# Cluster-routed attention with a SoLU feed-forward block: the same 1,568 operations recorded in another order

## The chip, the cores and the metric

The kernel runs on one core of a Trainium2 chip. The metric is the device time of one execution in microseconds, given as the median of three runs. Beside these runs stands one profiled execution, from which all durations, waits and starts below are read.

## The reference

Two stages follow each other. With B = 4 batches, H = 8 heads, S = 768 tokens and D = 64 the first is

```python
q_assign = argmax(normalised q . normalised centroids)      # 16 clusters a head
k_assign = argmax(normalised k . normalised centroids)
mask = q_assign[:, :, :, None] == k_assign[:, :, None, :]
scores = where(mask, scale * q @ k^T, -1e9)
attn = softmax(scores) @ v
```

Its output, 3072 tokens of 512 numbers, goes through the second:

```python
h = x @ w_in                          # 512 -> 1024
solu = h * softmax(h)
ln = (solu - mean) / sqrt(var + 1e-6) * g_ln
out = ln @ w_out                      # 1024 -> 512
```

## The kernel before, in words

**Scores.** The mask is put into the score matmul: under the 64 rows of q and of k stand the one-hot rows of the clusters, so that a pair of tokens in one cluster gets a constant more. One operation S r.x (L641) fills one of the two 512-column banks of a score tile `sb`; E r (ACT, L651) takes the exponent of both, 128x1024 at once. There are 144 regions r. V n.j (L663) multiplies six 128x128 blocks of exponents by v and by a column of ones into `ob`; N g (DVE, a reciprocal at L675 and a product at L686) normalises a group of these sums into the rows x of the second stage.

**Preparation of a pair of heads, b.p.** Loads of q and k (`ld`, SP) and v (`lv`); the transposes: for batch 0 by PE (`tp`, L396) with copies out of the banks on ACT or DVE (`xa`, `xt`, L407 and L409), for the others on DVE (`xt`, L421, 128x768); the products with the centroids on PE (`cl`, L470), turned back on DVE (`tb`, L479), their maximum (`mx`, L489), the one-hot comparison (`oh`, L493) and its transpose (`ot`, L500 and L505); the placing of the one-hot rows under q and k (`pl`, L529 and L531), the casts of q and k into their wide tiles (`ca`, L437 to L441, on POOL or ACT), the blank of unused rows (`bl`, L543), the cast of v (`cv`, L554 and L556).

**Feed-forward, tile f of 24.** `tx` (an SP transpose by DMA; PE for the first two and the last tile, `ptx`, L747) turns 128 rows of x. `h f.f2.part` (L772) fills the two banks `hb`, two matmuls of 512 columns each; `hm` (DVE, L782) takes a bank out with its running maximum; `ex` (ACT, L798) is the exponent; `u` (POOL or DVE, L805) is the product of exponent and h; `tu` (SP, L811) turns it by DMA; `bn` (DVE, L816, two a tile), `as` (L835) and `ag` (DVE, L821 and L823) make the variance; `al` (POOL, L840) its power -1/2. `y f.part` (L844) fills the one bank `mb`, four parts of two matmuls; `sc` (ACT, L856, or DVE, L858) scales the bank into the output tile, and `ou` stores it. Since `mb` is one bank, y of the next tile waits for `sc` of this one. The weights w_in come in by `li` (SP, into three staging buffers) and are cast by `wi` (POOL, L580); `ce` centres w_out.

**What sets the order.** Each operation is recorded under a name with what it needs. Two tables at the top of the file decide the rest: `AWAY` puts some operations on another engine than the usual one, and `ORDER` lists all names in the order in which `Weave.run` emits them. Each engine runs its own instructions in that order and waits by semaphore for what they need. Nothing else reorders the work; SP's queue too, with its loads, DMA transposes and stores, is one line in which a waiting entry holds up those behind it.

Of the kernel before, what the change touches and what calls it, by code (L numbers as in the profile page):

```python
# [38 lines left out]
lc ld0.0.0.0 ld0.0.1.0 ld0.0.0 ld0.0.1 ld0.1.0 ld0.1.1 lv0.0 ld0.2.0 ld0.2.1 ld0.3.0 lo3 lv0.1  # L39
ld0.3.1 lg lv0.2 lo1 lo2 lo0 cx z5 cy cz wu tp0.0.0.0 tp0.0.0.1 tp0.0.1.0 tp0.0.1.1 cp xa0.0.0  # L40
xt0.0.0 xa0.0.1 xt0.0.1 tp0.1.0.0 xa0.1.0 cb cl0.0 tb0.0 mx0.0 oh0.0 ot0.0 ca0.0.0.0.0 z3
ca0.0.1.0.0 ca0.0.0.0.1 cc ca0.0.0.1.1 ca0.0.0.1.0 pl0.0.1.1 pl0.0.0.0 ca0.0.1.0.1 ca0.0.1.1.1
ca0.0.1.1.0 tp0.1.0.1 tp0.1.1.0 xt0.1.0 xa0.1.1 cl0.0.1 tp0.1.1.1 cv0.0.1 xt0.1.1 pl0.0.0.1
tp0.2.0.0 tp0.2.0.1 tb0.0.1 mx0.0.1 oh0.0.1 ot0.0.1 pl0.0.1.0.1 pl0.0.1.0.0 pl0.0.1.1.1 cl0.1 sg
pl0.0.1.1.0 z1 ca0.1.1.0 cv0.0.0 ca0.1.0.0 xa0.2.0 pl0.0.1.0 tp0.2.1.0 xt0.2.0 xa0.2.1 S0.0 S0.1
E0 tp0.2.1.1 xt0.2.1 S1.0 tp0.3.0.0 S1.1 S2.0 S2.1 tp0.3.0.1 tb0.1 mx0.1 oh0.1 xa0.3.0 E1 E2 cl0.2
xt0.3.0 S3.0 S3.1 V0.0 V0.1 V1.0 S4.0 S4.1 V1.1 tp0.3.1.0 tb0.2 E3 S5.0 S5.1 E4 E5 ot0.1 N0 mx0.2
gt tp0.3.1.1 S6.0 S6.1 V2.0 V2.1 S7.0 S7.1 V3.0 V3.1 xa0.3.1 gk xt0.3.1 cl0.3 E6 E7 cv0.1.0
pl0.1.1.1 ca0.1.0.1 ca0.3.0.0 pl0.1.1.0 ca0.3.0.1 z2 ca0.1.1.1 oh0.2 pl0.1.0.0 pl0.1.0.1 gw S8.0
S8.1 S9.0 S9.1 me0 me1 ot0.2 tb0.3 pl0.2.1.0 N1 pl0.2.0.0 mx0.3 mk oh0.3 ca0.2.0.0 ca0.2.1.0  # L50
ca0.3.1.0 ca0.2.1.1 pl0.2.1.1 pl0.2.0.1 E8 E9 ca0.2.0.1 S10.0 S10.1 S11.0 S11.1 V4.0 V4.1 V5.0
V5.1 E10 S12.0 S12.1 cv0.2.1 E11 E12 mf N2 ot0.3 pl0.3.0.0 ld1.0.0.0 li0 ld1.0.0.1 ld1.0.0.2
ld1.0.0 ld1.0.1.0 lv0.3 ld1.0.1.1 ld1.0.1.2 ld1.0.1 cv0.1.1 ca0.3.1.1 pl0.3.1.0 pl0.3.0.1 cv0.2.0
cv0.3.0 cv0.3.1 wi0 S13.0 S13.1 V6.0 V6.1 S14.0 S14.1 V7.0 V7.1 pl0.3.1.1 N3 km ce0 E13 E14 S15.0
S15.1 S16.0 S16.1 E15 E16 V8.0 V8.1 S17.0 S17.1 E17 V9.0 V9.1 S18.0 S18.1 E18 S19.0 S19.1 N4 ce5
# [1299 lines left out]
```

## Time and profile before

| what | value |
|---|---|
| median of 3 runs | 222.03 us (221.85 to 222.12) |
| the profiled execution | 222.33 us |
| its span | 220.5 us |
| instructions | 6292 |
| HBM read and written | 23.11 MB and 6.29 MB |

The span runs from the first to the last recorded instruction; 1.83 us of the profiled execution lie around it. A start such as 42.81 is counted from the start of the span. In rows of a timeline stand the start, the length, the engine, the line, the operation, what it writes and reads, and in brackets the time for which the engine stood idle before it with the work that ended this. In rows of the chain of waits stand start, length and what the chain passes through. PE stands for TensorE, DVE for VectorE, ACT for ScalarE, POOL for GpSimd, SP for SyncE. The lengths of neighbours on one engine overlap a little, so a row of several operations (x2, x13) gives the pace at which they follow each other.

### The profile page before, as it was taken

How to read it: one execution, taken by the hardware profiler on the slowest of the kernel's cores; microseconds unless marked ns; L12 is line 12 of the kernel's file. 1: busy time of each engine (PE TensorE's matmuls, PEld its weight loads, DVE VectorE, ACT ScalarE, POOL GpSimd, SP SyncE). 2: the span in 40 equal slices, each digit the busy share in tenths (PEclk: the TensorE clock that was granted, in tenths of full speed). 3: DMA queues.
4: the chain of work that ended last, by engine and by line, in shares of the span. 5: the costliest groups of instructions: out<-in, count | busy, mean ns of one | idle time of the engine just before them, and what ended most of it. 6: DMA issues, size and time to landing. Idle time of an engine off the chain costs nothing.

```text
span 220.5 us, 6292 instructions
## 1 busy us (share of the span) xinstructions
PE 211.4 (96%) x2401; PEld 148.9 (68%) x2431; DVE 185.7 (84%) x430; ACT 192.8 (87%) x245; POOL 158.8 (72%) x198
## 2 busy tenths in 40 slices
PE   7899999999999999999999999999999999999984
PEld 4567577677678776777677677666777767655442
DVE  3699979968999999896799999994888856989982
ACT  3799999999999998999999989999999888685362
POOL 3686969897898999549939997879889054456610
PEclk9999999999999999999999999999999999999999
DMA  5998999999999993999999981939584229777522
GB/s 199 394 402 259 189 175 300 126 154 259 164 154 169 190 188 62 174 248 210 153 225 162 180 184 38 171 92 209 151 173 90 72 64 168 154 120 170 163 94 100
DMA packets 120911, 38.33 MB, mean 174 GB/s; under 512 B 109993, under 2 KB 116401, under 8 KB 120881
## 3 DMA queue, kind: packets, MB, share of 16 engines
q1 hardware_dynamic: 120448, 37.40, 81.7%
q10 hardware_dynamic: 432, 0.52, 0.7%
q8 instruction: 19, 0.31, 0.6%
q14 instruction: 12, 0.09, 0.2%
HBM read 23.11 MB, written 6.29 MB: 133 GB/s over the span
## 4 chain that ended last, share of the span: by engine, by line
PE 72%; DVE 10%; DMA 6%; POOL 5%; issue 3%; ACT 2%; SPq 1%; DVEq 0%; ACTq 0%; POOLq 0%
PE sb L641 22%; PE hb L772 16%; PE mb L844 15%; PE ob L663 12%; DMA w_st<-in_moe_w_in_dram 4%; PE hb L470 3%; DMA raw<-in_q_dram 2%; DVE w_st L782 2%; PE hb L396 2%; DVE xt L421 2%; DVE bs L816 2%; POOL kbig L441 1%; PE mb L470 1%; POOL w_in_sb L580 1%; POOL v L556 1%
## 5 line engine op out<-in xcount | busy, mean ns | idle before, releaser
L651 ACT ACTIVATE e<-sb 128x1024 bf16<-128x1024 f32 x144 | 139.9, 1024 | 8.9 <-PE sb L641 8.1
L641 PE MATMUL sb<-qbig,kbig 80*128 80x256 bf16 (+3 forms) x648 | 83.8, 261 | 1.3 <-ACT e L651 1.0
L641 PEld LDWEIGHTS <-kbig 80*128 80x128 bf16 (+1 forms) x648 | 62.9, 119 | 25.4 <-issue 8.6
L805 POOL TENSOR_TENSOR u<-e_sb,w_st 128x1024 bf16<-128x1024 bf16 x21 | 45.1, 2145 | 20.0 <-ACT e_sb L798 13.3
L663 PEld LDWEIGHTS <-e 128*128 128x128 bf16 x1152 | 48.6, 97 | 10.4 <-DVE x L686 0.6
L663 PE MATMUL ob<-v,e 128*128 128x65 bf16 x1140 | 51.4, 193 | 0.2
L772 PE MATMUL hb<-w_in_sb,xT 128*128 128x512 bf16 x173 | 50.6, 379 | 0.9 <-POOL v L1323 0.3
L844 PE MATMUL mb<-w_out_c,uT 128*128 128x512 bf16 x165 | 45.5, 379 | 1.2 <-DVE y L858 0.4
L816 DVE BATCH_NORM_STATS2 bs<-u 128x6 f32<-128x512 bf16 x48 | 31.6, 680 | 1.1 <-POOL u L805 1.1
L798 ACT ACTIVATE e_sb<-w_st,nmax 128x1024 bf16<-128x1024 f32 (+1 forms) x25 | 27.8, 1113 | 3.2 <-DVE w_st L782 1.8
L439 POOL CAST qbig<-xt 64x768 bf16<-64x768 f32 (+1 forms) x31 | 25.7, 830 | 6.5 <-PE ob L663 2.7
L441 POOL TENSOR_SCALAR kbig<-xt 64x768 bf16<-64x768 f32 (+1 forms) x32 | 27.6, 865 | 2.4 <-DVE xt L409 0.8
L840 POOL TENSOR_TENSOR alpha<-var,halves 128x1 f32<-128x1 f32 x24 | 15.3, 638 | 12.6 <-DVE var L823 8.0
L421 DVE STREAM_TRANSPOSE xt<-raw 128x768 f32<-128x768 f32 x24 | 22.5, 959 | 0.1
L844 PEld LDWEIGHTS <-uT 128*128 128x128 bf16 x176 | 15.2, 97 | 10.2 <-issue 0.8
L772 PEld LDWEIGHTS <-xT 128*128 128x128 bf16 x192 | 15.8, 98 | 8.8 <-issue 0.6
L686 DVE TENSOR_TENSOR x<-ob,den 128x256 bf16<-128x256 f32 (+2 forms) x40 | 19.0, 474 | 1.4
L782 DVE TENSOR_SCALAR_CACHE_REDUCE w_st<-hb 128x512 f32<-128x512 f32 x24 | 16.3, 680 | 3.8 <-PE hb L772 3.7
L782 DVE TENSOR_SCALAR_CACHE_REDUCE w_st<-hb,nmax 128x512 f32<-128x512 f32 x24 | 17.8, 740 | 1.9 <-PE hb L772 1.5
L856 ACT ACTIVATE y<-mb,alpha 128x512 f32<-128x512 f32 x15 | 10.3, 685 | 6.5 <-POOL alpha L840 3.6
L675 DVE RECIPROCAL den<-ob 128x4 f32<-128x4 f32 (+2 forms) x40 | 7.1, 178 | 10.4 <-PE ob L663 10.1
L556 POOL CAST v<-vf 128x384 bf16<-128x384 f32 x22 | 10.9, 504 | 3.3 <-DMA vf<-in_v_dram 2.6
(109 smaller groups left out, 202.6 us busy)
## 6 DMA issues: line engine op xcount, KB each, us to landing
vf<-in_v_dram SPq DMA_DIRECT2D x16, 384.0 KB, 5.3
out_dram<-y SPq DMA_DIRECT2D x23, 256.0 KB, 2.5
raw<-in_k_dram SPq DMA_DIRECT2D x26, 192.0 KB, 4.6
raw<-in_q_dram SPq DMA_DIRECT2D x24, 192.0 KB, 5.1
w_g<-in_moe_w_out_dram SPq DMA_DIRECT2D x4, 512.0 KB, 8.7
w_st<-in_moe_w_in_dram SPq DMA_DIRECT2D x4, 512.0 KB, 8.0
raw<-in_q_dram SPq DMA_DIRECT2D x3, 384.0 KB, 6.6
...
```

The costliest lines, as they stand in the source:

```text
L421: nc.vector.transpose(xts[b, p, i][:], raw_of(b, p, i))
L439: (nc.vector if e == "DVE" else nc.gpsimd).tensor_copy(dst, src)
L441: (nc.vector if e == "DVE" else nc.gpsimd).tensor_scalar(dst, src, scalar1=inv_C, scalar2=1.0, op0=Alu.mult, op1=Alu.mult)
L641: nc.tensor.matmul(reg[:, c:c + wd], kb[u, pp, side_of(h), keys], qb[u, pp, side_of(h), su * P:su * P + wd])
L651: nc.scalar.activation(es[r][:, :w], src, Act.Exp, scale=exp_scale, bias=-exp_scale)
L663: nc.tensor.matmul(ops_of(group_of[n])[:, s, :VW], es[r][:, c0:c0 + P], v1[index[b, pair_of(h)] % R][:, side_of(h), kt, :VW], start=(kt == ...
L772: nc.tensor.matmul(hb[f2][:], xTs[f][:, dc, :], w_in_sb[:, dc, f2 * BANK:(f2 + 1) * BANK], start=(dc == 0), stop=(dc == n_dc - 1))
L782: nc.vector.tensor_scalar(ff[f, "h"][:, f2 * BANK:(f2 + 1) * BANK], hb[f2][:], scalar1=-1.0, scalar2=nmax[:, f2 - 1:f2] if f2 else 3.0e38, ...
L798: nc.scalar.activation(ff[f, "e"][:, cols(f, f2)], ff[f, "h"][:, cols(f, f2)], Act.Exp, bias=ff[f, "nmax"][:, n_ff2 - 1:], scale=-1.0, acc ...
L805: (nc.vector if e == "DVE" else nc.gpsimd).tensor_tensor(ff[f, "u"][:, cols(f, f2)], ff[f, "e"][:, cols(f, f2)], ff[f, "h"][:, cols(f, f2) ...
L816: nc.vector.bn_stats(ff[f, "bs"][:, f2, :], ff[f, "u"][:, f2 * BANK:(f2 + 1) * BANK])
L844: nc.tensor.matmul(y_of(f, x), ff[f, "uT"][:, fc, :], w_out_c[:, fc, parts_of(f, x)], start=(fc == 0), stop=(fc == n_fc - 1))
```

## The change

The two tables are replaced; all 1,568 operations, their buffers and their instructions stay. By `AWAY`, DVE has 296 operations instead of 301, ACT 216 instead of 219, POOL 191 instead of 183; PE (722) and SP (143) are as they were. In detail: of `pl`, 12 go from DVE to POOL and 5 back, 2 from ACT to POOL and 2 back, and one each way between ACT and DVE; of `cv`, 6 go from ACT to POOL and 4 back; of `ca`, 3 from ACT to POOL and one back; of `as`, 9 from DVE to POOL and 10 back; of `sc`, 3 from ACT to DVE and 4 back; of `u`, u14 and u20 go from DVE to POOL, u10, u13 and u16 back; of `bl`, one goes to POOL and two to DVE. The `ORDER` table is new throughout. A line of it before, and two of now (the scalings of tile 9 and what stands around them):

```diff
-S117.0 E116 S117.1 E117 V76.0 h15.0.0 h15.0.1 S118.0 S118.1 V76.1 ot3.2 sc9 u13.0 pl3.2.1.1
+ca3.2.0.1 pl3.2.0.1 cv3.2.0 S115.0 S115.1 S116.0 S116.1 h14.1.0 h14.1.1 V75.0 y9.1 E115 ex13.0
+E116 V75.1 V76.0 V76.1 y9.2 y9.3 S117.0 S117.1 S118.0 S118.1 V77.0 h15.0.0 E117 E118 sc9 y10.0
```

The tables of the changed kernel have one line less, so that its lines read one lower than before (L641 is L640). Three places follow, as they stand on the engine.

**ACT ahead of the first exponent.** Before, from the copy xa0.1.0 (the first transpose of pair 0.1) to E0. The cast to `kbig` is ca0.0.1.1.0, the cast to `v_0` is cv0.0.1; L529 are placings.

```order
L407 COPY xt<-hb_92 128x384
L437 ACTIVATE kbig_99<-xt 64x2x3x64
L407 COPY xt<-hb_93 128x384
L407 COPY xt<-hb_92 128x384
L554 CAST v_0_102<-vf 128x6x64
L407 COPY xt<-hb_93 128x384
L529 COPY qbig_96<-oht 32x6x32
L407 COPY xt<-hb_92 128x384
L529 COPY kbig_99<-oht 32x6x32
```

Now, from the same copy:

```order
L406 COPY xt<-hb_92 128x384
L406 COPY xt<-hb_93 128x384
L406 COPY xt<-hb_92 128x384
L406 COPY xt<-hb_93 128x384
L528 COPY qbig_96<-oht 32x6x32
L406 COPY xt<-hb_92 128x384
L528 COPY qbig_96<-oht 32x6x32
```

The two casts have left this stretch for POOL, and ca0.0.1.0.0, which POOL did, now stands on ACT three rows earlier. On SP, the loads of q and k of pair 0.2 now stand ahead of the first load of v, the last load of v ahead of the first of w_in, and li2, which stood behind li1 and li3, ahead of both; the one that takes the buffer freed by the cast wi0 is then li3.

**DVE around the scaling of tile 9.** Before, from N30 (the reciprocal and the product, 6x64) to `sc9` (L858) and three rows on:

```order
L675 RECIPROCAL den<-ob 128x6
L686 TENSOR_TENSOR x<-ob,den 128x6x64
L816 BN_STATS bs<-u 128x6
L500 STREAM_TRANSPOSE oht<-oh 128x768
L858 TENSOR_SCALAR y<-mb,alpha 128x512
L821 BN_AGGR mv<-bs 128x2
L823 TENSOR_SCALAR var<-es_2777,esum,mv 128x1
L816 BN_STATS bs<-u 128x6
```

Now, from hm14.0, two rows behind N30 (between them stands hm13.1), to `sc9` (L857):

```order
L781 TENSOR_SCALAR w_st,nmax<-hb_92 128x512
L834 TENSOR_SCALAR es_2911<-esum 128x1
L542 MEMSET kbig_100 16x2x384
L815 BN_STATS bs<-u 128x6 x2
L820 BN_AGGR mv<-bs 128x2
L822 TENSOR_SCALAR var<-es_2630,esum,mv 128x1
L820 BN_AGGR mv<-bs 128x2
L822 TENSOR_SCALAR var<-es_2783,esum,mv 128x1
L820 BN_AGGR mv<-bs 128x2
L822 TENSOR_SCALAR var<-es_2900,esum,mv 128x1
L815 BN_STATS bs<-u 128x6
L857 TENSOR_SCALAR y<-mb,alpha 128x512
```

Between N30 and `sc9` stand hm13.1, hm14.0, as12, bl3.2, bn11 twice, ag9, ag10, ag11 and bn12.0, where before there were bn10.1 and ot3.2. The last of them reads u12, which POOL makes.

**DVE ahead of the products with the centroids of pairs 3.2 and 3.3.** These are sixteen matmuls on PE, of which the last (cl3.3) reads the transpose xt3.3.1. Before, from the normalising N27 (4 columns):

```order
L675 RECIPROCAL den<-ob 128x4
L686 TENSOR_TENSOR x<-ob,den 128x2x2x64
L835 TENSOR_SCALAR es_2642<-esum 128x1
L421 STREAM_TRANSPOSE xt<-raw 128x768
L531 COPY qbig_96<-oht 32x4x192
L421 STREAM_TRANSPOSE xt<-raw 128x768 x3
```

Now, from the same N27:

```order
L674 RECIPROCAL den<-ob 128x4
L685 TENSOR_TENSOR x<-ob,den 128x2x2x64
L781 TENSOR_SCALAR w_st,nmax<-hb_92 128x512
L820 BN_AGGR mv<-bs 128x2
L822 TENSOR_SCALAR var<-es_2495,esum,mv 128x1
L781 TENSOR_SCALAR w_st,nmax<-hb_93,nmax 128x512
L420 STREAM_TRANSPOSE xt<-raw 128x768 x3
```

One transpose, one small operation and one placing have left the stretch, and hm11 of both banks and ag8 have come in.

More of the change, by code (lines that the diff above doesn't have):

```diff
@@ L35 @@
+    u8.0 u9.0
 """.split(), "POOL"))
 ORDER = """
[L39 to L55, printed above, removed]
@@ new lines @@
+h21.0.1 y17.0 y17.1 y17.2 hm20.1 ex20.0 S141.0 S141.1 E141 h21.1.0 y17.3 S142.0 S142.1 h21.1.1
+S143.0 S143.1 sc17 as18 ag18 as19 al18 hm21.0 hm21.1 E142 E143 ex21.0 y18.0 V94.0 bn19.0 as20
+y18.1 V94.1 y18.2 h22.0.0 h22.0.1 y18.3 sc18 u20.0 u21.0 bn19.1 bn20.0 bn20.1 N39 ag19 ag20 hm22.0
+h22.1.0 V95.0 V95.1 h22.1.1 hm22.1 ex22.0 al19 as21 u22.0 y19.0 ptx23.0 tx23.0 N40 y19.1 y19.2
+y19.3 ptx23.1 h23.0.0 h23.1.0 ou17 tu20 ou18 tu21 bn21.0 tx23.1 bn21.1 al20 h23.0.1 sc19 y20.0
+y20.1 y20.2 y20.3 sc20 h23.1.1 ou19 hm23.0 ag21 bn22.0 hm23.1 ptu22.0 ptu22.1 tu22.1 bn22.1 ex23.0
```

198 lines of the change are left out of this document (103 added, 95 removed).

## The prediction

> **What bounds the kernel now.** First the page's busy times:
>
> ```profile
> PE 211.4 (96%) x2401; PEld 148.9 (68%) x2431; DVE 185.7 (84%) x430; ACT 192.8 (87%) x245; POOL 158.8 (72%) x198
> ```
>
> then the same by stretches of the span:
>
> ```profile
> 12.00:45.00 33.00, 31.57 (x416) 22.66 (x414) 28.91 (x60) 32.17 (x39) 27.06 (x39) 1.00 1.01 236
> 45.00:85.00 40.00, 39.68 (x502) 30.03 (x506) 37.42 (x81) 39.28 (x47) 35.78 (x40) 1.00 1.01 174
> 125.00:165.00 40.00, 39.58 (x430) 28.30 (x437) 35.24 (x77) 37.91 (x49) 33.91 (x38) 1.00 0.77 144
> 165.00:205.00 40.00, 39.62 (x458) 26.73 (x463) 31.64 (x88) 31.52 (x41) 21.73 (x22) 1.00 0.59 123
> ```
>
> The columns behind the window are PE, its weight loads, DVE, ACT, POOL, the granted clock (1.00 throughout), DMA. In the three rows behind 45 us PE lacks 0.3 to 0.4 us of each 40: no reordering can win much there, only a new hole can lose. The others are busy for 85 to 98% in the rows up to 165 us, so a row that is moved back on DVE or ACT has little room. From 12 to 45 us ACT is busy for 32.17 of 33 us. There ACT bounds, as its timeline shows:
>
> ```profile
> 12.99 1.02 ACT L651 ACTIVATE e<-sb 128x1024 bf16<-128x1024 f32 x1
> ...
> 26.63 12.27 ACT L651 ACTIVATE e<-sb 128x1024 bf16<-128x1024 f32 x13
> 39.10 1.94 ACT L651 ACTIVATE e<-sb 128x1024 bf16<-128x1024 f32 x2 [0.19 <-PE sb L641]
> ...
> 43.94 10.76 ACT L651 ACTIVATE e<-sb 128x1024 bf16<-128x1024 f32 x11 [0.22 <-PE sb L641]
> ```
>
> Exponents follow each other at 12.27 / 13 = 0.94 us; from E0 at 12.99 to 54.7 the timeline names two holes, 0.19 and 0.22. So the time up to there is E0's start plus ACT's work. What sets E0 is read from the chain of waits in the first microseconds, followed back from a matmul at 20 us:
>
> ```profile
> 7.94 0.48 ACT xt L407
> ...
> 8.44 0.52 ACT kbig L437
> 8.96 0.77 ACT xt L407 x2
> ...
> 9.76 0.52 ACT v L554
> ...
> 10.37 0.88 PE hb L396 x6
> ```
>
> The reader is to see the two casts (ca0.0.1.1.0, cv0.0.1) inside the chain: PE's transposes of pair 0.2 at 10.37 stand behind them.
>
> **The change part by part.** The sum is made against the profiled execution, 222.33 us; the median, 222.03, lies 0.30 lower, and the result is moved by that.
>
> *ACT ahead of E0.* Both casts leave this stretch. The 0.52 and 0.52 don't come back whole: xt0.1.0 also needs its own transpose on PE, and DVE's second round of one-hots keeps its place. Carried on: xa0.1.0 ends at 8.42, xt0.1.0 can start at some 8.65, then xa0.1.1 and xt0.1.1 at about 0.45 each (0.77 for two in the chain); the transposes of pair 0.2 start at about 10.05 for 10.37. I take **-0.35**; the ends are 0 (DVE's chain is late instead) and -1.0 (both casts). What POOL gets, it has idle time for (72% busy), and the v cast isn't needed before the first values matmul. Since ACT has no hole behind E0, the gain lasts to 54.7 us.
>
> *The hole at 43.94.* PE stood before it, and behind a weight load:
>
> ```profile
> 41.72 1.04 POOL L580 CAST w_in_sb<-w_st 128x1024 bf16<-128x1024 f32 x1 [0.80 <-DMA w_st<-in_moe_w_in_dram]
> ...
> 42.81 0.38 PE L772 MATMUL hb<-w_in_sb,xT 128*128 128x512 bf16 x1 [0.33 <-POOL v L1323]
> ```
>
> The first row is the cast wi2, released by a load; PE's second matmul of h0.0.1 begins when it is done. (The releaser named, a small fill on POOL, is the one behind the cast.) The chain of waits of the whole span passes here:
>
> ```profile
> 29.84 1.85 issue
> ...
> 33.68 7.99 DMA w_st<-in_moe_w_in_dram
> ```
>
> That load, 7.99 us from 33.68, is li2, the last of three, waiting for the buffer that wi0 frees, while wi0 stood behind a late v load (the 1.85 without work in POOL's chain). Now the v load is ahead of w_in's first, and li2 goes first of the three; li3 takes the freed buffer, with the same 7.99 us from about 31, thus at 39 us. The wait goes: **-0.2**, ACT's hole of 0.22 (ends 0 and -0.4, both holes).
>
> *y2.0.* Tile 2's first matmul waited for sc1, which stood on DVE behind two transposes:
>
> ```profile
> 85.32 0.71 DVE L858 TENSOR_SCALAR y<-mb,alpha 128x512 f32<-128x512 f32 x1
> 86.08 0.38 PE L844 MATMUL mb<-w_out_c,uT 128*128 128x512 bf16 x1 [0.36 <-DVE y L858]
> ```
>
> Now sc1 stands right behind ag2 and N16 and y2.0 later: **-0.35** (ends 0 and -0.5).
>
> *y10.0.* Here a wait comes. What ran there, from the timeline:
>
> ```profile
> 155.99 0.75 DVE L858 TENSOR_SCALAR y<-mb,alpha 128x512 f32<-128x512 f32 x1 [0.67 <-PE mb L844]
> 156.66 0.20 DVE L821 BATCH_NORM_AGGREGATE mv<-bs 128x2 f32<-128x12 f32 x1
> ...
> 157.09 0.68 DVE L816 BATCH_NORM_STATS2 bs<-u 128x6 f32<-128x512 bf16 x1
> ...
> 157.90 0.59 PE L844 MATMUL mb<-w_out_c,uT 128*128 128x512 bf16 x2
> ```
>
> and the pace of work that runs back to back, from the chain of waits:
>
> ```profile
> 64.35 0.56 PE ob L663 x18
> ...
> 69.05 0.66 DVE w_st L782 x2
> ...
> 71.81 0.70 DVE kbig L543
> ...
> 75.86 1.20 DVE bs L816 x2
> ...
> 78.27 1.83 DVE xt L421 x2
> ...
> 88.85 0.44 PE sb L641 x4
> ...
> 98.74 0.86 PE hb L772 x4
> ```
>
> Before, sc9 ran at 155.99 as soon as PE was done, over 1 us ahead of y10.0 at 157.90. Now DVE has, behind the end of h14.0.1: hm14.0 0.66, as12 0.07 (an estimate, half a row), bl3.2 0.70, bn11 1.20, three ag at 157.09 - 156.66 = 0.43, bn12.0 0.60, sc9 0.75; with 0.2 to start (an estimate) and 0.05 to release PE (sc1 ended at 86.03 above, PE began at 86.08), 5.5 us. In the new table PE has in the same time h14.1, y9.1 to y9.3 and h15.0.0 (12 matmuls at 0.215), S115 to S118 (16 at 0.11) and V75 to V77.0 (30 at 0.03): 2.58 + 1.76 + 0.9 = 5.2. Difference **+0.3**. Ends: 0, and +1.0 where u12, which bn12.0 reads, is late too.
>
> *cl3.3.* From the end of V67 DVE has N27 (0.56, rows below), hm11 of both banks (1.32), ag8 0.43, three transposes at 0.91, and 0.2 to start: 5.25 us. PE has S103 to S106 (1.76), y7 (8 at 0.215, 1.72), V68 and V69 (24, 0.72) and cl3.2 (0.78): 4.95 us.
>
> ```profile
> 139.96 0.14 DVE L675 RECIPROCAL den<-ob 128x4 f32<-128x4 f32 x1
> 140.14 0.42 DVE L686 TENSOR_TENSOR x<-ob,den 128x256 bf16<-128x256 f32 x1
> ...
> 139.25 1.68 PE L470 MATMUL hb<-xt,c_bd 128*32 128x384 f32 x16
> ```
>
> (0.78 is half of the 16 products' pace.) **+0.3** (ends 0 and +0.6).
>
> *ptx23.1.* PE's last transpose of x waits for N40. From the end of h21.1.1 DVE has hm21.1, bn19 and bn20, N39, ag19, ag20, hm22, a copy and N40: by the same paces 0.66 + 2.4 + 0.45 + 0.86 + 1.32 + 0.3 + 0.45 and 0.3 for starts, 6.75 us, for 6.55 of PE (y18, h22 and y19, 24 matmuls, 5.16; S143, V94, V95 and a transpose, 1.4). Before, N40 stood two rows behind N39, ag19, ag20 and hm22 as well, but bn19 and bn20 were done by then.
>
> **+0.2** (ends 0 and +0.6). Behind it hm23.1 now stands ahead of bn22.1 (0.6 us), but y22 waits for ACT's copy, which now stands behind the exponents of tile 23: 0.
>
> *What isn't listed.* Some fifteen other places (y4.0, y14.0, S53 to S80, V66) come out within 0.1 us of PE's work, as many did before; I take **+0.3** for them, at 0.02 each, with ends -0.3 and +1.0. For DMA transposes and stores I found none whose new place on SP uses up its lead: 0.
>
> Sum: -0.35 - 0.2 - 0.35 + 0.3 + 0.3 + 0.2 + 0.3 = **+0.2**, so 222.53 for the profiled execution and **222.3 us** as a median.
>
> **The rivals.** *No new wait bites.* The three DVE chains start earlier than I have them, or rows overlap more; then only the first three terms count: -0.9, thus 221.1. For it: all three excesses are at most 0.3 us, near what these paces can tell. Against: DVE is busy for 88 and 94% of the two rows up to 165 us, with little idle time to start early from.
>
> *ACT bounds throughout.* ACT loses two casts of q or k net, two of v, and gets one scaling more:
>
> ```profile
> 41.06 0.84 ACT L437 ACTIVATE qbig<-xt 64x768 bf16<-64x768 f32 x1
> ...
> L856 ACT ACTIVATE y<-mb,alpha 128x512 f32<-128x512 f32 x15 | 10.3, 685 | 6.5 <-POOL alpha L840 3.6
> ```
>
> With 0.51 for a cast of v (9.76 in the chain above): -1.68 - 1.02 + 0.69 = -2.0, thus 220.0. Against: from 125 to 165 us ACT is idle for 2.1 us of 40, PE for 0.4. The Trainium skill, "Perfetto Trace Analysis", section "Identifying the Most-Contended Engine", says to judge PE by its weight loads (68% here) and not by matmul time, which would make ACT (87%) the engine to relieve. The stretches speak against it: score matmuls follow at 0.11 us without a gap while the weight loads stand at 30 of 40.
>
> *POOL is late for sc9.* That is the other side: sc9 now stands behind bn12.0, which waits for u12. POOL has ahead of it two casts, u11, a placing and u12:
>
> ```profile
> 153.14 2.14 POOL L805 TENSOR_TENSOR u<-e_sb,w_st 128x1024 bf16<-128x1024 bf16 x1
> ```
>
> u12 ended at 155.28. y10.0 stands at 157.9; less sc9, its release and bn12.0 (1.4 us), u12 decides from 156.5 on. POOL has eight operations more than before, and a cast of q or k holds it for 0.8 us each, as one took on ACT (41.06 above). With 1.0 more at y10.0 the time is 223.3. That engines slow each other is seen: the comparison `oh` of one size took
>
> ```profile
> 62.58 1.55 DVE L493 TENSOR_TENSOR oh<-cst,mx 128x768 bf16<-128x768 f32 x1
> 147.39 0.95 DVE L493 TENSOR_TENSOR oh<-cst,mx 128x768 bf16<-128x768 f32 x1
> ```
>
> in two places, 0.6 us apart. The Trainium skill, "SBUF — State Buffer", section "SBUF: two separate sides", has VectorE (in operations with two SBUF inputs) and GpSimd lock one port pair for a whole instruction; by that rule work moved to POOL holds DVE up as well, and this rival would be the likelier one.
>
> *The order doesn't matter.* PE hides all of it: 222.0.
>
> **How the numbers follow.** Forecast 0.44, between 221.8 and 222.8; no new wait 0.18; ACT bound 0.04; POOL late 0.27; no matter 0.07. A measurement tells 0.2%, 0.44 us, from no change. Faster than that: 0.18 + 0.04 and 0.03 of the forecast's own = 0.25. Within it: 0.07 and 0.26 of the forecast = 0.33. Slower: 0.27 and 0.15 of the forecast (the unlisted places at their upper end) = 0.42. The range goes from the no-wait rival, 221.0, to POOL late with the upper ends of the other two DVE chains, 223.3 + 0.7 = 224.0.
>
> **What would show it.** Right: E0 starts at about 12.6; no PE wait at h0.0.1 and y2.0; new PE waits of 0.2 to 0.5 on DVE at y10.0, cl3.3 and ptx23.1. Wrong: E0 at 13.0 or later; a wait of 1 us at y10.0 with u12's end behind 156.5; PE waiting on a DMA behind 45 us.

## The result, and the profile after

| | before | after |
|---|---|---|
| median of 4 runs each, on one chip | 222.07 us (221.85 to 222.16) | 223.84 us (223.43 to 224.57) |
| ratio | | 1.0086, 95% interval 1.0066 to 1.0107 |
| profiled execution, its span | 222.33, 220.5 us | 223.43, 221.7 us |

The new order is slower by 1.8 us, and by 1.1 us between the two profiled executions. The forecast was 222.3 us within 221.0 to 224.0; the sign with the larger chance came true, the size did not.

The busy times of the page and the same four stretches as before hide this well:

```profile
PE 213.2 (96%) x2431; PEld 147.8 (67%) x2431; DVE 182.4 (82%) x425; ACT 191.0 (86%) x242; POOL 162.0 (73%) x206
```

```profile
12.00:45.00 33.00, 31.96 (x423) 22.91 (x424) 29.64 (x63) 32.00 (x39) 27.29 (x37) 1.00 1.02 247
45.00:85.00 40.00, 40.00 (x495) 29.25 (x494) 37.86 (x79) 38.95 (x46) 33.79 (x38) 1.00 0.94 172
...
125.00:165.00 40.00, 39.16 (x428) 27.43 (x424) 35.26 (x82) 36.48 (x47) 31.81 (x37) 1.00 0.74 129
165.00:205.00 40.00, 40.00 (x468) 26.56 (x466) 27.37 (x77) 32.96 (x43) 20.41 (x20) 1.00 0.61 133
```

DVE and ACT have less to do than before, PE is at 40.00 of 40 in two rows, and yet the kernel is slower. The one row that became worse is 125 to 165 us: PE 39.16 for 39.58, ACT 36.48 for 37.91. PE lost more than these two numbers say. In before the trace has 2401 of the 2431 matmuls, and the 0.42 us that PE lacks in this row are eight holes of 0.05 us where a matmul's record is missing; in after all are there, and the 0.84 us are three waits (0.32, 0.15 and 0.37, below). A matmul that waits is partly counted as busy, so even this is only a part. What shows the rest is the start of the same operation in two traces. Four marks serve all kernels below: E0, E33 and E100 (exponents on ACT, where both orders have done nearly the same work) and the second matmul of y23.1.3, directly ahead of y23.0.0, which is among the last matmuls.

| profiled execution | E0 | E0 to E33 | E33 to E100 | E100 to y23.1.3 | span |
|---|---|---|---|---|---|
| before | 12.99 | 35.91 | 82.41 | 84.84 | 220.5 |
| after | 12.90 | 35.32 | 82.50 | 86.53 | 221.7 |
| blank_pool | 13.54 | 36.03 | 82.50 | 85.58 | 222.1 |
| place_dve | 12.58 | 36.04 | 82.48 | 86.35 | 221.9 |
| u10_pool | 13.01 | 36.04 | 82.48 | 85.97 | 221.9 |
| tail_norm | 13.22 | 35.99 | 82.49 | 87.07 | 223.2 |
| ce_later | 12.62 | 35.31 | 83.07 | 86.66 | 222.0 |
| pool_quiet | 12.89 | 35.30 | 82.97 | 86.52 | 222.1 |
| before_ce2 | 12.82 | 35.75 | 82.41 | 84.84 | 220.2 |
| hybrid | 12.83 | 35.43 | 82.29 | 84.99 | 219.9 |
| front_only | 12.43 | 36.03 | 82.47 | 84.96 | 220.3 |
| y10_only | 13.09 | 35.58 | 82.42 | 86.84 | 222.3 |
| tail_only | 12.69 | 36.11 | 82.41 | 85.11 | 220.7 |
| y10_three | 13.36 | 36.02 | 82.49 | 85.69 | 222.0 |

Between before and after: -0.09, -0.59, +0.09 and +1.69, together +1.10. In these two executions the front gained what it was to gain, 0.67 us by E33; behind E100 more than twice as much was lost. In most other profiled executions of this front it gained nothing from E0 to E33, as is told below under the collision.

**The front.** ACT's timeline, after:

```profile
8.81 0.86 ACT L406 COPY xt<-hb 128x384 f32<-128x384 f32 x2 [0.46 <-PE hb L395]
...
12.90 1.02 ACT L650 ACTIVATE e<-sb 128x1024 bf16<-128x1024 f32 x1
...
34.91 3.78 ACT L650 ACTIVATE e<-sb 128x1024 bf16<-128x1024 f32 x4 [0.39 <-ACT e L650]
38.99 1.94 ACT L650 ACTIVATE e<-sb 128x1024 bf16<-128x1024 f32 x2 [0.30 <-PE sb L640]
...
41.70 12.46 ACT L650 ACTIVATE e<-sb 128x1024 bf16<-128x1024 f32 x13
```

The two casts are gone, but in their place ACT waits 0.46 us for PE's transposes, and E0 came only 0.09 earlier. The last row is 13 exponents without a hole: the wait of 0.22 at 43.94 is gone, since the load that it hung on is. POOL's timeline has the cast wi2 in a row of three that starts at 37.33, where before it waited 0.80 us for its load and ran at 41.72:

```profile
37.33 3.01 POOL L579 CAST w_in_sb<-w_st 128x1024 bf16<-128x1024 f32 x3
```

**Tile 2 and pair 3.3.** PE's timeline at y2.0 and at the products with the centroids:

```profile
84.28 0.60 PE L843 MATMUL mb<-w_out_c,uT 128*128 128x512 bf16 x2
...
138.35 1.74 PE L469 MATMUL hb<-xt,c_bd 128*32 128x384 f32 x16
```

y2.0 has no bracket behind it any more: its wait is gone. The sixteen products took 1.74 for 1.68 us; the wait for DVE's last transpose, which lies inside this row, is the same in both orders.

**Around y10.0.** First DVE's timeline, after:

```profile
146.21 1.21 DVE L804 TENSOR_TENSOR u<-e_sb,w_st 128x1024 bf16<-128x1024 bf16 x1
...
152.16 0.68 DVE L781 TENSOR_SCALAR_CACHE_REDUCE w_st<-hb 128x512 f32<-128x512 f32 x1
...
153.93 0.70 DVE L542 MEMSET kbig<- 16x768 f32 x1 [1.00 <-ACT kbig L528]
154.64 1.29 DVE L815 BATCH_NORM_STATS2 bs<-u 128x6 f32<-128x512 bf16 x2
...
157.11 0.68 DVE L815 BATCH_NORM_STATS2 bs<-u 128x6 f32<-128x512 bf16 x1
157.71 0.73 DVE L857 TENSOR_SCALAR y<-mb,alpha 128x512 f32<-128x512 f32 x1
```

and one row of the same engine before, at the same operation hm14.0 as the second row above:

```profile
152.45 0.69 DVE L782 TENSOR_SCALAR_CACHE_REDUCE w_st<-hb 128x512 f32<-128x512 f32 x1 [2.54 <-PE hb L772]
```

Before, DVE stood idle for 2.54 us here, waiting for PE's h14.0.1. After, hm14.0 comes as promptly behind it, but the idle time has been filled, with u10 (1.21, which POOL did before) among others, and the statistics that could have gone ahead now stand behind. In between bl3.2, which blanks rows behind the placings of its tile, waits 1.00 us for the placing pl3.2.1.0, which is on ACT now; sc9, the last row, ends at 158.44. ACT and PE, after:

```profile
149.72 1.15 ACT L797 ACTIVATE e_sb<-w_st,nmax 128x1024 bf16<-128x1024 f32 x1 [0.68 <-POOL u L804]
...
152.81 0.83 ACT L528 COPY kbig<-oht 32x768 f32<-32x768 f32 x1
```

```profile
151.65 0.38 PE L771 MATMUL hb<-w_in_sb,xT 128*128 128x512 bf16 x1
...
152.84 0.60 PE L640 MATMUL sb<-qbig,kbig 96*128 96x256 bf16 x4 [0.32 <-ACT e L650]
...
156.92 0.60 PE L640 MATMUL sb<-qbig,kbig 80*128 80x256 bf16 x4 [0.15 <-ACT e L650]
...
158.50 0.59 PE L843 MATMUL mb<-w_out_c,uT 128*128 128x512 bf16 x2 [0.37 <-DVE y L857]
```

The first row is the end of h14.0.1, 152.03. From there to y10.0 PE waits three times, at S116.1, S118.1 and y10.0. The brackets count only idle time; by the starts of the matmuls the three cost 0.48, 0.32 and 0.53 us, 1.33 together. Before, the timeline of PE names no wait between 152 and 162 us. What bounds this stretch is read from the other end: from h14.0.1's end to sc9's the queue on DVE takes 6.41 us (152.03 to 158.44), and PE's own work up to y10.0 is 5.21. The difference, 1.20, is what PE must lose whatever it waits for in between, so that the two waits on ACT cost nothing of their own here.

**The tail.** PE's timeline at ptx23.1:

```profile
207.57 0.23 PE L746 MATMUL sb<-ident_b,x 128*128 128x128 bf16 x1 [0.17 <-DVE x L685]
```

### The profile page after: what moved, and what is told of

Same layout as the page of the kernel before. It is cut to its first block, busy times and chain, and to the rows that moved or that the text cites. A ratio compares the mean times of both kernels' runs of the same rounds, so it can differ in the third digit from the quotient of the medians.

```text
span 221.7 us, 6295 instructions
## 1 busy us (share of the span) xinstructions
PE 213.2 (96%) x2431; PEld 147.8 (67%) x2431; DVE 182.4 (82%) x425; ACT 191.0 (86%) x242; POOL 162.0 (73%) x206
## 4 chain that ended last, share of the span: by engine, by line
PE 74%; ACT 13%; DVE 5%; issue 3%; DMA 2%; POOL 1%; SPq 0%; DVEq 0%; POOLq 0%; ACTq 0%
PE sb L640 23%; PE hb L771 16%; PE mb L843 14%; PE ob L662 13%; ACT e L650 10%; PE hb L469 4%; DMA raw<-in_k_dram 2%; DVE bs L815 2%; ACT e_sb L797 2%; PE hb L395 1%; ACT xt L406 1%; DVE w_st L781 1%; POOL u L804 1%; PE mb L469 1%; DVE y L857 1%
## 5 line engine op out<-in xcount | busy, mean ns | idle before, releaser
L640 PE MATMUL sb<-qbig,kbig 80*128 80x256 bf16 (+3 forms) x648 | 81.3, 261 | 1.5 <-ACT e L650 1.3
L640 PEld LDWEIGHTS <-kbig 80*128 80x128 bf16 (+1 forms) x648 | 63.0, 119 | 25.8 <-issue 10.0
L804 POOL TENSOR_TENSOR u<-e_sb,w_st 128x1024 bf16<-128x1024 bf16 x20 | 43.1, 2155 | 17.3 <-ACT e_sb L797 12.6
L662 PEld LDWEIGHTS <-e 128*128 128x128 bf16 x1152 | 48.0, 97 | 9.8 <-issue 0.8
L771 PE MATMUL hb<-w_in_sb,xT 128*128 128x512 bf16 x192 | 52.7, 379 | 0.0
L662 PE MATMUL ob<-v,e 128*128 128x65 bf16 x1140 | 50.7, 193 | 0.0
L843 PE MATMUL mb<-w_out_c,uT 128*128 128x512 bf16 x176 | 48.3, 379 | 0.6 <-DVE y L857 0.4
L839 POOL TENSOR_TENSOR alpha<-var,halves 128x1 f32<-128x1 f32 x24 | 14.7, 619 | 16.2 <-DVE var L822 15.7
L843 PEld LDWEIGHTS <-uT 128*128 128x128 bf16 x176 | 14.6, 97 | 10.3 <-issue 1.0
L530 POOL COPY qbig<-oht 32x768 f32<-32x768 f32 (+1 forms) x15 | 11.5, 768 | 5.3 <-DVE oht L499 4.5
L855 ACT ACTIVATE y<-mb,alpha 128x512 f32<-128x512 f32 x16 | 11.0, 690 | 4.9 <-POOL es L834 2.5
```

The costliest lines, as they stand in the source:

```text
L640: nc.tensor.matmul(reg[:, c:c + wd], kb[u, pp, side_of(h), keys], qb[u, pp, side_of(h), su * P:su * P + wd])
L662: nc.tensor.matmul(ops_of(group_of[n])[:, s, :VW], es[r][:, c0:c0 + P], v1[index[b, pair_of(h)] % R][:, side_of(h), kt, :VW], start=(kt == ...
L771: nc.tensor.matmul(hb[f2][:], xTs[f][:, dc, :], w_in_sb[:, dc, f2 * BANK:(f2 + 1) * BANK], start=(dc == 0), stop=(dc == n_dc - 1))
L804: (nc.vector if e == "DVE" else nc.gpsimd).tensor_tensor(ff[f, "u"][:, cols(f, f2)], ff[f, "e"][:, cols(f, f2)], ff[f, "h"][:, cols(f, f2) ...
L843: nc.tensor.matmul(y_of(f, x), ff[f, "uT"][:, fc, :], w_out_c[:, fc, parts_of(f, x)], start=(fc == 0), stop=(fc == n_fc - 1))
```

## The experiments

Each kernel is after with one edit, if nothing else is said; the edits are lines of the two tables. Ratios are against before, timed on the same chip. Executions of one kernel differ by their E0 (12.4 to 13.5 us in the table, with no relation to the order) and by a collision that is told below.

### Three placements around y10.0, each undone alone

**blank_pool**: bl3.2 from DVE back to POOL, where it was before.

```diff
-    as1 as10 as12 as13 as15 as16 as17 as20 as23 as3 as5 as6 as7 as8 bl1.0 bl1.2 bl3.2 ce0 ce2
+    as1 as10 as12 as13 as15 as16 as17 as20 as23 as3 as5 as6 as7 as8 bl1.0 bl1.2 ce0 ce2
```

> The changed kernel with one engine changed: the blank bl3.2 is on POOL, not on DVE. Theory A (one chain costs the time around y10.0: u10 on DVE makes hm12.1 late, so ex12 and E114 are late; the placing pl3.2.1.0 behind E114 on ACT is what bl3.2 waits for on DVE, 1.00 us, and ag9, sc9 and y10.0 stand behind bl3.2): DVE's wait of 1.00 us at 152.9 is gone, sc9 starts at about 156.1 instead of 157.7, PE's wait at y10.0 (0.53 between matmuls) is gone, the two waits for exponents ahead of it (0.48 and 0.32) stay: 0.5 us less than the changed kernel, about 223.3. Rival B (POOL's load holds DVE up): POOL gets 0.7 us more, sc9 gains less than 0.5 us, time unchanged or up to 0.5 us more. Rival C (the loss is spread over many small waits): under 0.2 us either way.

Measured: 223.14 us, ratio 1.0035 (1.0010 to 1.0061). E100 to y23.1.3 took 85.58, 0.95 less than after; 0.42 of this is not bl3.2's but comes of `oh`, the one-hot comparison of pair 3.2, which was not held up in this execution (told at y10_three and in the last section). With bl3.2 its wait has left DVE too: the queue from h14.0.1 to sc9 takes 4.73 us, less than PE's 5.21, and y10.0 waits no more. What is left are 0.47 us, of which 0.31 is the wait on ACT at S118.1, now in the open.

**place_dve**: pl3.2.1.0 from ACT back to DVE.

```diff
-    cv3.3.1 pl0.0.0.0 pl0.0.0.1 pl1.2.1.0 pl3.2.1.0 xa0.0.0 xa0.1.0 xa0.1.1 xa0.2.0 xa0.2.1
+    cv3.3.1 pl0.0.0.0 pl0.0.0.1 pl1.2.1.0 xa0.0.0 xa0.1.0 xa0.1.1 xa0.2.0 xa0.2.1
-    pl1.0.1.0 pl1.2.1.1 pl2.0.0.0 sc0 sc1 sc11 sc15 sc3 sc4 sc9
+    pl1.0.1.0 pl1.2.1.1 pl2.0.0.0 sc0 sc1 sc11 sc15 sc3 sc4 sc9 pl3.2.1.0
```

> The changed kernel with the placing pl3.2.1.0 on DVE, as it was before, instead of ACT. Theory A: DVE does 0.55 us of work where it waited 1.00 us, so sc9 starts 0.4 to 0.5 us earlier and PE's wait at y10.0 falls from 0.53 to about 0.1; ACT is freed of 0.83 us ahead of E115, so the wait of 0.32 us for E116 goes; the one for E114 (0.48) stays: 0.7 us less than the changed kernel, about 223.1. Rival B: nothing changes on POOL, and the gain is that of ACT alone, 0.3. Rival C: under 0.2 us.

Measured: 224.01 us, ratio 1.0062 (1.0039 to 1.0085); E100 to y23.1.3 86.35, 0.18 less than after, where 0.7 was expected. Both waits on ACT are gone, and the one at y10.0 has grown from 0.53 to 1.08 us: PE's timeline of this kernel has

```profile
158.71 0.59 PE L843 MATMUL mb<-w_out_c,uT 128*128 128x512 bf16 x2 [0.92 <-DVE y L857]
```

The work only changed queues: DVE does the placing in the place of waiting for it, and its queue takes 6.24 us for 6.41. Here too `oh` was not held up. Against tail_norm below, which has that as well and whose queue takes 6.00 us, this placing made the queue longer by 0.24.

**u10_pool**: u10 from DVE back to POOL.

```diff
-    u8.0 u9.0
+    u8.0 u9.0 u10.0
```

> The changed kernel with the product u10 on POOL, as it was before, instead of DVE. Theory A: DVE loses 1.2 us ahead of hm12.1, ACT's hole of 0.68 us ahead of ex12 goes, E113 and E114 come 0.6 to 0.7 us earlier, and with them pl3.2.1.0, bl3.2 and sc9: PE's waits for E114 (0.48) and E116 (0.32) go, and that at y10.0 (0.53) falls below 0.2: 1.0 to 1.3 us less than the changed kernel, about 222.7. Rival B: POOL does 2.1 us more in the stretch, u11 and u12 come later by 1 us or more, bn12.0 and sc9 with them, and y10.0 waits longer: no gain or up to 1 us more. Rival C: under 0.2 us.

Measured: 223.32 us, ratio 1.0040 (1.0014 to 1.0065); E100 to y23.1.3 85.97, 0.56 less, where 1.0 to 1.3 was expected. The queue takes 5.63 us, and the wait ahead of bl3.2 is what changed, in DVE's timeline of this kernel:

```profile
153.96 0.70 DVE L542 MEMSET kbig<- 16x768 f32 x1 [0.20 <-issue]
```

The first link lies at u10, but it does not go by hm12.1, as theory A has it. In after hm12.1 was done at 148.81, and ex12, the exponent of tile 12 on ACT, started only at 149.72, behind the 0.68 us above. Its bracket names a product on POOL, which is u11. POOL's timeline, after:

```profile
146.39 1.08 POOL L834 TENSOR_SCALAR es<-esum 128x1 f32<-128x1 f32 x1 [2.65 <-ACT e_sb L797]
147.55 2.14 POOL L804 TENSOR_TENSOR u<-e_sb,w_st 128x1024 bf16<-128x1024 bf16 x1
```

u11, the second row, ends at 149.69, and ex12 starts 0.03 us later, as it does in blank_pool, place_dve, tail_norm, ce_later and pool_quiet. Ahead of u11 stands as11, the first row: an operation on 128 numbers, which took 1.08 us while u10 ran on DVE (146.21 to 147.42) and takes 0.19 here. So u10 on DVE held up POOL, and u11 on POOL held up ACT; the placing behind ex12 and bl3.2 follow in turn. Counted from E100, ex12 starts at 19.01 us in after, at 18.59 where `oh` is not held up (tail_norm) and at 18.17 here, without a wait and 0.15 us ahead of u11's end. Why ex12 needs u11 in after and not here, the traces don't show.

### The tail

**tail_norm**: four statistics behind the copy tx23.1, which brings the last turned part of x out of its bank. (Before, only one of the four, bn21.0, stood there.)

```diff
-y18.1 V94.1 y18.2 h22.0.0 h22.0.1 y18.3 sc18 u20.0 u21.0 bn19.1 bn20.0 bn20.1 N39 ag19 ag20 hm22.0
+y18.1 V94.1 y18.2 h22.0.0 h22.0.1 y18.3 sc18 u20.0 u21.0 bn19.1 N39 ag19 hm22.0
-y19.3 ptx23.1 h23.0.0 h23.1.0 ou17 tu20 ou18 tu21 bn21.0 tx23.1 bn21.1 al20 h23.0.1 sc19 y20.0
+y19.3 ptx23.1 h23.0.0 h23.1.0 ou17 tu20 ou18 tu21 tx23.1 bn20.0 bn20.1 ag20 bn21.0 bn21.1 al20 h23.0.1 sc19 y20.0
```

> The changed kernel with bn20 (twice), ag20 and bn21.0 moved on DVE from ahead of N39 and hm22 to behind N40 and the copy tx23.1. Theory A (N40 is late because 1.7 us of statistics stand ahead of it on DVE): N40 starts at about 206.3 instead of 207.0, PE's wait at ptx23.1 (0.45 us by its neighbours) is gone, and what follows moves with it: 0.4 us less than the changed kernel. Rival: N40 waits for hm22.1 and the matmuls ahead of it anyway, or al20 and sc20 now come late and y21.0 waits as long: under 0.15 us.

Measured: 224.71 us, ratio 1.0090 (1.0059 to 1.0121), the slowest of all, where 0.4 us less than after was expected; E100 to y23.1.3 87.07, 0.54 more than after. PE's wait at ptx23.1 is gone:

```profile
207.80 0.22 PE L746 MATMUL sb<-ident_b,x 128*128 128x128 bf16 x1
```

But the statistics now stand on DVE ahead of hm23.1, the last pass over tile 23, which started at 211.29 in after and in this kernel at

```profile
212.87 0.73 DVE L781 TENSOR_SCALAR_CACHE_REDUCE w_st<-hb,nmax 128x512 f32<-128x512 f32 x1
```

Counted from ptx23.1, hm23.1 starts 1.35 us later (5.07 for 3.72), for 0.3 us saved at ptx23.1. Since the stretch around y10.0 lost 0.42 less in this execution (`oh` again), the tail alone lost 0.96. Of the two places tried for these statistics, that of after is the better.

### A collision in the front

In after's profiled execution E0 to E33 took 35.32 us (35.58 to 36.11 in four traces with before's front); in the six other kernels with an unchanged front of after (blank_pool, place_dve, u10_pool, tail_norm, front_only, y10_three) it took 35.99 to 36.04. The difference is one place, DVE's two products for w_out (ce0, ce2). After, and then blank_pool, whose front is the same:

```profile
32.47 1.75 DVE L617 SCALAR_TENSOR_TENSOR w_out_c<-w_g,g_ln,y 128x512 bf16<-128x512 f32 x2
```

```profile
33.16 2.76 DVE L617 SCALAR_TENSOR_TENSOR w_out_c<-w_g,g_ln,y 128x512 bf16<-128x512 f32 x2
```

The second is 1.01 us longer; N5 behind it comes later, the sums wait for its bank and the exponents for the scores. In ACT's timeline of blank_pool the holes are

```profile
37.76 2.01 ACT L650 ACTIVATE e<-sb 128x1024 bf16<-128x1024 f32 x2 [0.21 <-PE sb L640]
40.35 1.94 ACT L650 ACTIVATE e<-sb 128x1024 bf16<-128x1024 f32 x2 [0.58 <-PE sb L640]
```

where after has 0.30 at one of them. Three kernels try to take the collision away.

**ce_later**: ce0 and ce2 behind N8, after POOL's ce6 is done.

```diff
-V11.1 S20.0 S20.1 S21.0 S21.1 E20 E21 li2 ce0 ce2 N5 ptx0 li1 li3 ld1.2.0.0 ld1.2.0.1 ld1.2.0.2
+V11.1 S20.0 S20.1 S21.0 S21.1 E20 E21 li2 N5 ptx0 li1 li3 ld1.2.0.0 ld1.2.0.1 ld1.2.0.2
-S30.0 S30.1 E29 E30 hm0.0 N8 V18.0 h0.1.1 S31.0 S31.1 V18.1 V19.0 S32.0 S32.1 V19.1 h1.0.0 oh1.0
+S30.0 S30.1 E29 E30 hm0.0 N8 ce0 ce2 V18.0 h0.1.1 S31.0 S31.1 V18.1 V19.0 S32.0 S32.1 V19.1 h1.0.0 oh1.0
```

> The changed kernel with ce0 and ce2 (two centring operations of w_out on DVE) moved from ahead of N5, where POOL works on ce6, to behind N8. Theory P (an operation of DVE with two inputs from SBUF and one of POOL don't run together, one of them stands still; ce0 and ce2 beside ce6 hold N5, and N5 holds the first transposes ptx0 on PE): PE's position against its own work, which falls back by 2.6 us between S20 and S40 in four executions of five and by 1.9 in one, falls back by 1.3 to 1.5, as before the change (1.35): 1.0 us less than the changed kernel in most executions. Rival Q (ACT's row of exponents sets that stretch, DVE's place in it does not matter): 2.6 stays, no change. Rival R (only the order on DVE counts, 1.4 us of work ahead of N5): the same gain, told apart by pool_quiet.

Measured: 223.74 us, ratio 1.0071 (1.0051 to 1.0091). The products took 0.74 and 0.75 us and E0 to E33 35.31, as wanted; E33 to E100 became 83.07, 0.57 longer, in two holes of ACT's timeline:

```profile
50.05 1.02 ACT L650 ACTIVATE e<-sb 128x1024 bf16<-128x1024 f32 x1 [0.18 <-PE sb L640]
51.70 2.90 ACT L650 ACTIVATE e<-sb 128x1024 bf16<-128x1024 f32 x3 [0.63 <-PE sb L640]
```

The products now hold up DVE's one-hots of pair 1.0, whose placing S36 needs.

**pool_quiet**: POOL's ce6 and ce1 behind its casts wi2, wi1, wi3.

```diff
-N6 V14.0 V14.1 V15.0 V15.1 z5 ce6 ce1 wi2 wi1 wi3 tb1.0 tb1.1 N7 mx1.0 ca1.0.0.0 ca1.0.1.1 S26.0
+N6 V14.0 V14.1 V15.0 V15.1 z5 wi2 wi1 wi3 ce6 ce1 tb1.0 tb1.1 N7 mx1.0 ca1.0.0.0 ca1.0.1.1 S26.0
```

> The changed kernel with ce6 and ce1 on POOL moved behind its three casts wi2, wi1 and wi3, so that POOL has nothing to do beside ce0 and ce2; DVE's order stays. Theory P: ce0 and ce2 take 0.75 us each instead of 1.08 and 1.77, N5 starts 1.2 to 1.4 us earlier against N4, the fall-back between S20 and S40 shrinks from 2.6 to at most 1.9 us: 0.7 us less or more, unless ce6 and ce1, now at 40 to 44 us, hold the casts of pair 1.0 for S36. Rival R (order on DVE alone): ce0 and ce2 keep their lengths or the fall-back stays at 2.6. Rival Q: no change.

Measured: 223.91 us, ratio 1.0074 (1.0058 to 1.0090). Again 0.74 and 0.75, E0 to E33 35.30, and E33 to E100 82.97. With both, what the collision cost came back as a wait 15 us later. They show that it can be avoided, not that this is worth anything in this order.

**before_ce2**: the other way about, before with ce2 directly behind ce5 (15 us earlier on DVE).

```diff
-S15.1 S16.0 S16.1 E15 E16 V8.0 V8.1 S17.0 S17.1 E17 V9.0 V9.1 S18.0 S18.1 E18 S19.0 S19.1 N4 ce5
+S15.1 S16.0 S16.1 E15 E16 V8.0 V8.1 S17.0 S17.1 E17 V9.0 V9.1 S18.0 S18.1 E18 S19.0 S19.1 N4 ce5 ce2
-S28.1 E28 V16.0 V16.1 V17.0 S29.0 S29.1 h0.1.0 V17.1 S30.0 S30.1 E29 E30 oh1.0 hm0.0 N8 ot1.0 ce2
+S28.1 E28 V16.0 V16.1 V17.0 S29.0 S29.1 h0.1.0 V17.1 S30.0 S30.1 E29 E30 oh1.0 hm0.0 N8 ot1.0
```

> The kernel before with one operation moved: ce2 on DVE goes from behind the transpose ot1.0 (46.9 us) to directly behind ce5, ahead of N5 and beside ce6 on POOL. Theory P: ce2 takes 1.1 to 1.8 us there, N5 and ptx0 come 1.1 us or more later, and the fall-back between S20 and S40 grows from 1.35 to 2 to 2.6: 0.6 to 1.2 us slower than before. Rival Q: within 0.2 us of before.

Measured: 222.48 us, ratio 1.0004 (0.9990 to 1.0018): ce2 took 1.17 us for 0.71, and nothing came of it (E0 to E33 35.75 us), where theory P had 0.6 to 1.2 us more. Half a microsecond more for ce2 costs nothing at this place.

### The order cut into stretches

Since nearly everything behind E33 and outside these places repeats to some 0.03 us, the two orders can be joined at names where both have issued the same work.

**hybrid**: after's order and placements where it gains, before's elsewhere.

```
after to S21.1 | before to S40.0 | after to S104.1 | before to the end
```

> The order of after up to S21.1, then that of before up to S40.0, then that of after up to S104.1, then that of before to the end; each operation on the engine that its part gives it. By the positions of PE against its work in the profiles, the first part of after gains 0.36 us between S0 and S20, the third gains 0.7 us (0.48 from S40 to S65, and 0.25 up to S104), and the losses of after lie in the second and the fourth: 1.0 us less than before, about 221.2, if the terms add up and the seams cost nothing. Rival (each order is good only as a whole): a wait at a seam of 0.3 us or more, and no gain on before.

Measured: **221.71 us** (221.39 to 222.47, 12 runs), ratio 0.9974 (0.9961 to 0.9987): faster than both kernels, and than before by 0.66 us (222.37 in the runs beside it), where 1.0 was expected. E0 to E33 35.43, where before's order has 35.58 to 36.11 (before, before_ce2, y10_only, tail_only), since ACT's row is after's and ce2, at 46.30, is out of the collision; E33 to E100 82.29 for 82.41; E100 to y23.1.3 84.99, as in before. Behind E100 DVE again has before's slack, at hm14.0 and at sc9:

```profile
151.80 0.69 DVE L781 TENSOR_SCALAR_CACHE_REDUCE w_st<-hb 128x512 f32<-128x512 f32 x1 [2.55 <-PE hb L771]
...
155.34 0.75 DVE L857 TENSOR_SCALAR y<-mb,alpha 128x512 f32<-128x512 f32 x1 [0.67 <-PE mb L843]
```

**front_only**, **y10_only** and **tail_only** take one stretch of after each:

```
front_only: after to S104.1 | before to the end
y10_only:   before to S104.1 | after to S130.0 | before to the end
tail_only:  before to S130.0 | after to the end
```

> The order of after up to S104.1 (136 us), the order and engines of before from there. Theory P (the losses are local and add up): the front part alone gains what the exponent row shows, E100 0.59 us earlier in after than in before, so 221.6 to 221.8 us where before is 222.2 to 222.4; where ce0 and ce2 meet ce6 (1.08 and 1.75 us in place of 0.74 and 1.10) that gain is lost again and the time is 222.4 to 222.6. Theory Q (the front's gain is swallowed later, since the transfers and vector work behind 136 us have their own pace): as before within 0.2 us.

> The order of before up to S104.1, that of after up to S130.0, that of before again to the end: only u10.0 and bl3.2 on DVE, pl3.2.1.0 on ACT, and the order around y10.0, are new. Theory P: PE falls back by 1.3 to 1.6 us between S104 and S143 more than in before, 223.5 to 223.9 us, the S115 to S120 stretch at about +1.5. Theory Q (this stretch loses only because the front brought it forward: ACT and POOL would have been late for it anyhow): within 0.5 us of before, 222.2 to 222.7.

> The order of before up to S130.0 (174 us), that of after from there: h23.0.0 behind bn20, the late N39 and N40. Theory P: +0.5 us at h23.0.0 and -0.25 at y23.0.0, so 222.4 to 222.7 us. Theory Q (h23.0.0 is late in after only because PE is late): as before within 0.2 us.

Measured: front_only 222.42 us, ratio 1.0002 (0.9982 to 1.0022); y10_only 224.15 us, ratio 1.0085 (1.0061 to 1.0109); tail_only 222.41 us, ratio 1.0002 (0.9981 to 1.0022). The middle stretch alone, in a kernel that is otherwise before, loses as much as the whole change: E100 to y23.1.3 86.84, +2.00. Theory Q, that it is late only because the front brought it forward, doesn't hold. But the total says more than its parts: at y10.0 itself 0.63 us were lost (a queue of 5.63 us, bl3.2 waiting 0.20), while PE lost 0.55 at 141 us, waiting for POOL, and 0.89 at 178, the last at the joint to before's order. The run shows that this stretch of the new order costs time without the new front, not how much of it at y10.0. The tail alone costs 0.27 (85.11 - 84.84) in its one trace; its time does not tell this from nothing.

The front is the least clear of the three. Its profiled execution met the collision (ce0 and ce2 1.08 and 1.76 us, E0 to E33 36.03), as theory P has it for a time of 222.4 to 222.6; the median agrees, but its interval does too with theory Q's "as before".

**y10_three**: the three placements undone together (the diffs of blank_pool, place_dve and u10_pool in one).

> After with u10.0 on POOL, bl3.2 on POOL and pl3.2.1.0 on DVE as in before, the order kept. Each alone left +0.58, +0.74 and +1.35 us in the stretch S115 to S120 where after has +1.52. Theory P1 (three separate waits): all three away bring it to 0 to +0.2, 222.2 to 222.5 us. Theory P2 (one chain, in which POOL's or DVE's own work is what is late once one of the three is moved): +0.5 to +0.8, about 223.0 us. The dispute of oh3.2 and ca3.1.0.0 (1.6 us in place of 0.95 or 0.82) stays in either.

Measured: 223.21 us, ratio 1.0043 (1.0026 to 1.0061); E100 to y23.1.3 85.69, 0.84 less than after. Alone the three gave 0.95, 0.56 and 0.18, but these can't be added up: they are links of one chain, and in the traces of blank_pool and place_dve `oh` took 0.95 us and not 1.59. With tail_norm, which has `oh` at 0.95 and none of the three edits, blank_pool lost 0.53 less and place_dve 0.24 more (last column below). The waits on ACT are gone, the one at y10.0 stays at 0.54 us:

```profile
158.82 0.59 PE L843 MATMUL mb<-w_out_c,uT 128*128 128x512 bf16 x2 [0.38 <-DVE y L857]
```

This is the outcome of theory P2: DVE has pl3.2.1.0 again (0.82) for bl3.2 (0.70), and the statistics are still ahead of sc9. The queue for all kernels with this stretch of after, with PE's own 5.21 us up to y10.0 and what PE lost from h14.0.1 to the matmul behind y10.0:

| kernel | h14.0.1's end to sc9's end | less 5.21 | PE lost |
|---|---|---|---|
| ce_later, pool_quiet | 6.43, 6.41 | 1.22, 1.20 | 1.43, 1.42 |
| after | 6.41 | 1.20 | 1.42 |
| place_dve | 6.24 | 1.03 | 1.24 |
| tail_norm | 6.00 | 0.79 | 1.00 |
| u10_pool | 5.63 | 0.42 | 0.64 |
| y10_only | 5.63 | 0.42 | 0.63 |
| y10_three | 5.58 | 0.37 | 0.59 |
| blank_pool | 4.73 | -0.48 | 0.47 |

Where the queue is longer than PE's work, PE loses the difference and 0.2 more, each time; where it is shorter, in blank_pool, ACT's waits set what is lost. In tail_norm nothing of this stretch was edited; what differs is a collision further up (`oh` at 0.95 us for 1.59, told in the last section). That the statistics (bn11, three ag and bn12.0, 3.1 us of the queue) would do no harm ahead of hm14.0 or behind sc9 was not tried alone; in hybrid, where ag9 stands ahead and bn11 and bn12.0 behind, PE does not wait there.

## Why the prediction was right or wrong

223.84 us lies inside the range, close to its upper end, and slower was the likeliest of the three outcomes. That it lies inside is in part luck: the upper end was u12 late by 1.0 us and two DVE chains at their worst, and none of this happened. The forecast of 222.3 is 1.5 us short, and most of that lies in one term, y10.0.

*PE lacks 0.3 to 0.4 us of each 40: misread.* In the three rows that the step names, all that PE lacks (0.32, 0.42 and 0.38 us) are holes of 0.05 us where a matmul's record is missing, 21 of the 30 that the page lacks against the weight loads. What was inferred, that only a new hole could matter much there, holds all the more.

*Ahead of E0, -0.35: wrong in its place, right in its sum by luck.* E0 came 0.09 earlier. The ends of the range had "0 (DVE's chain is late instead)"; it was PE's transposes that ACT waited for. Over all kernels E0 says nothing on the order: 12.69 to 13.09 with before's head, 12.43 to 13.54 with the new one. But ACT gains 0.34 between E0 and E15 (before 12.99 to 30.26, after 12.90 to 29.83), where the step expected nothing; the seven traces with the new front have 16.90 to 16.98 us there, those with before's 17.27 or more.

*The hole at h0.0.1, -0.2: right about the wait.* None is left there. At E33 after is 0.67 us ahead, for 0.55 forecast. What the wait was worth can't be told: E15 to E33 took 18.39 us after and 18.63 before, but 18.24 to 18.47 in the other traces with before's front.

*y2.0, -0.35: the wait went, the time did not.* E33 to E100 took 82.41 before and 82.50 after. That a wait of PE is not worth its length where ACT is at 38.95 of 40 us, since the exponents come no sooner, is argued and not shown. In hybrid, with this part of after's order, the stretch gave 0.12.

*cl3.3, +0.3: wrong.* The row grew by 0.06. The same wait was there before, inside the row of sixteen matmuls that the step read as pace.

*y10.0, +0.3 with an end of +1.0: the term that was too small, by one wait.* Its two sums were 5.5 us for DVE from h14.0.1's end to sc9's, and 5.2 for PE. PE's work is 5.21, and DVE did begin with hm14.0 at once (152.16 behind 152.03). DVE took 6.41: the 5.5 and bl3.2's 1.00 of waiting for ACT, less 0.1. The step counted bl3.2 at its 0.70 and named u12 as what might be late behind it; it never asked what bl3.2 itself waits for. That is pl3.2.1.0, which the change had sent to ACT behind ex12, and ex12 was late by POOL's as11 and u11, which u10 on DVE held up. Of bl3.2's 1.00, 0.4 is `oh`'s, which was held up further ahead (0.61 in tail_norm, where it was not). So the place and the mechanism (sc9 late by its queue on DVE, PE waiting at y10.0) were right, and the size was 1.3 us for 0.3 (1.42 here, of which before has 0.09 too). blank_pool, u10_pool and place_dve each change one link: the queue falls by bl3.2 and its wait (1.7), by most of the wait (0.8), and hardly, since 0.82 of work takes the wait's place.

*ptx23.1, +0.2: right.* The bracket is 0.17, 0.33 by the starts of the matmuls, and the stretch 0.27 in tail_only.

*The rivals.* "POOL is late for sc9" gave 223.3, nearest of the four, but its mechanism didn't happen: u12 started at 151.32 and was done at 153.47, 3 us ahead of the 156.5 from which it would decide. POOL was late in another place, at u11, for which ex12 waited.

```profile
151.32 2.14 POOL L804 TENSOR_TENSOR u<-e_sb,w_st 128x1024 bf16<-128x1024 bf16 x1
```

"ACT bounds throughout" falls too: ACT's busy time fell by 1.8 us (192.8 to 191.0) and the time rose. The forecast's +0.3 for what isn't listed can't be told apart from the stretches: E33 to E100 gave +0.09 in all, y2.0 included.

*The rest of the 1.8.* Of the 1.69 us lost behind E100, 1.33 stand at y10.0 and 0.27 in the tail. But the profiled executions differ by 1.10, the medians by 1.77. The collision of ce0 and ce2 costs 0.7 us in six of seven profiled executions of this front, and the one without it is after's own. It explains less than that of the missing 0.67, since in blank_pool, place_dve and tail_norm, which met it, `oh` was not held up, which gave 0.4 back. E0 alone differs by 1.1 us between executions, and place_dve's ten times fall into two groups (223.49 to 223.72 and 224.30 to 224.51), of which its trace, with the collision, belongs to the lower. So at least half of the 0.67 stays open; there is no second trace of after itself.
